# First chunk in halves of 64 times, own key's weight as a product, output banks from a second PSUM pool

## Chip, core and metric

One core of a Trainium2 chip runs the kernel. The metric is the device time of one execution in microseconds (us), the median of three runs. Besides, one execution was profiled; all rows below are from it.

## What is computed

Four sequences of 768 times with 8 heads of 48 channels go through a linear recurrence with a decaying state; the result goes, as 3072 tokens of 384 channels, through a two-layer network with a GELU between.

```
state = 0                                   # per batch and head, 48 x 48
for t in range(768):
    cur = (u * k[t]) outer v[t]             # the own key's weight is u
    y[t] = r[t] @ (state + cur)
    state = w[:, None] * state + k[t] outer v[t]
x = y as [3072, 384]
h = x @ w_in                                # 384 x 2048
out = (0.5 * h * (1 + erf(h / sqrt(2)))) @ w_out     # 2048 x 384
```

w_in and w_out come as 64-bit floats and are split on the chip into a high and a low part of 32 bits.

## The kernel before

**Tiling of the recurrence.** Time is cut into six chunks of 128. A chunk is four groups, one for each pair of heads; pair 3 comes first, since its channels fill the gaps of 16 rows in the other pairs' tiles (`x3`, `gaps`, `spread`). Within a chunk the recurrence is written as products: scores r times k with both sides scaled by powers of w, a mask that keeps past keys, the own key's weight on the diagonal, then the masked scores times v (`new`), r times the state (`old`), and the sum of k times v, weighted by powers of w, that updates the state (`gain`, `gains`).

**Two forms.** The first chunk (`first_group`, groups 0 to 3) takes all 128 times at once. It has no earlier state. Its tables `W` reach from w^-64 to w^64, with a reciprocal per pair (L271). T is scaled in up to two parts on VectorE (DVE) and GpSimd (POOL) (L393); r times k is formed per element (L399), summed per head with u by small products (`sum_pairs`, L404), brought out of PSUM (`cs`, L408) and put on the diagonal of `Am` by ScalarE (ACT), DVE or POOL (`bonus`, L351, L356); the scores (L419) are copied into `Am` where the mask says past (L425). `new` is L439, `gain` L445, and ACT copies the gain out as the state (L450). Groups 4 to 23 cut their 128 times into two halves of 64, each with its own state. They scale by `E` (L479), form r times k and times u on POOL (L482, L488), sum on DVE (L491), weight k by `WN2` on POOL (L485), and put the sums on the diagonals with eight ACT instructions (L351). `E` is filled from `W` by eight DMAs within SBUF (L303), because half 1 needs the heads of a pair swapped; `WN` and `WN2` are transposes by PE of two sets of powers (L290, L293).

```
def go():                  # one entry of PE's order per later group
    old()                  # r times state of the group before, into Y (L519)
    scores()               # scores of this group, into A (L527)
    gains()                # k times v of this group, into A beside the scores (L536)
    new()                  # masked scores times v of the group before, into Y (L546)
```

The state of a half is updated by DVE out of A (L569), the past scores are copied out of A (L576), and `keep` brings the output out of Y: ACT writes the high part (L367), DVE the low one (L368).

**The network.** 96 steps, 16 for each chunk of 512 tokens. In step m, `moe1` makes 128 hidden channels in bank `Hp` by nine products (high and low parts, L602), ACT applies GELU twice (L630, L631), DVE forms the low part (L632), and `moe2` of the step before adds nine products into the three output banks (L642). A pair of weights is loaded and split in the first 16 steps only (`w_split`: ACT L330, L332, L340; DVE L334, L336, L338, L342). The first `NEAR` weight tiles are there from the start; the others take the space of the first chunk's tiles, after `swap` has given back that pool.

**Order.** `Plan` holds every operation with its engine, a cost, a due time and what it reads and writes. It plays a model of the engines and fixes each engine's order before the program is built: of what is ready, the one due first. DMAs all go through the queue of SP. While PE would sit idle ahead of the first hidden product, the plan fills in products of zeros (`heat`), which keep its clock up.

**PSUM.** Eight banks: A (2), Y and U (one tile of 2 banks), Hp, and three output banks O. In the first chunk even groups use A and Y, odd ones O.

## Time and profile before

| what | value |
|---|---|
| median of three runs | 513.9 us (512.32, 513.9, 517.1) |
| the profiled execution | 512.43 us |
| its span, first to last instruction | 510.7 us |
| mean granted TensorE clock | 0.973 of 2.4 GHz |
| busy, share of the span | PE 96%, PEld 76%, DVE 49%, ACT 42%, POOL 17% |

PE is TensorE's products, PEld its weight loads, SPq the queue of SyncE that issues DMAs. A share of busy time is a mean over stages with different limits; the rows below go by stage. Products are pipelined, and the records of two that overlap both count, so a busy PE is not PE at its peak.

### The profile page before, as it was taken

How to read it: one execution, taken by the hardware profiler on the slowest of the kernel's cores; microseconds unless marked ns; L12 is line 12 of the kernel's file. 1: busy time of each engine (PE TensorE's matmuls, PEld its weight loads, DVE VectorE, ACT ScalarE, POOL GpSimd, SP SyncE). 2: the span in 40 equal slices, each digit the busy share in tenths (PEclk: the TensorE clock that was granted, in tenths of full speed). 3: DMA queues.
4: the chain of work that ended last, by engine and by line, in shares of the span. 5: the costliest groups of instructions: out<-in, count | busy, mean ns of one | idle time of the engine just before them, and what ended most of it. 6: DMA issues, size and time to landing. Idle time of an engine off the chain costs nothing.

```text
span 510.7 us, 10489 instructions
## 1 busy us (share of the span) xinstructions
PE 488.2 (96%) x4524; PEld 387.8 (76%) x4524; DVE 248.8 (49%) x363; ACT 213.6 (42%) x472; POOL 88.6 (17%) x80
## 2 busy tenths in 40 slices
PE   5998898999999999999999999999999999999995
PEld 4876676766778778787777778778778787888884
DVE  8959999998536424614425435424424311211111
ACT  2458758774444243333343443343442322322221
POOL 5850311213022022202022022022022000000000
PEclk8659999999999999999999999999999999999998
DMA  8864574822402303403302403303403000100001
GB/s 226 254 251 145 189 231 149 252 83 63 145 7 89 94 4 92 145 1 94 95 1 94 142 5 94 94 1 94 134 13 94 13 0 12 62 1 0 1 0 67
DMA packets 15107, 45.04 MB, mean 88 GB/s; under 512 B 3728, under 2 KB 4112, under 8 KB 15056
## 3 DMA queue, kind: packets, MB, share of 16 engines
q1 hardware_dynamic: 15056, 44.32, 27.8%
q8 instruction: 37, 0.61, 0.5%
q14 instruction: 14, 0.11, 0.1%
HBM read 37.16 MB, written 4.72 MB: 82 GB/s over the span
## 4 chain that ended last, share of the span: by engine, by line
PE 84%; DVE 11%; issue 2%; ACT 1%; DMA 1%; SPq 0%; DVEq 0%
PE Hp L602 37%; PE O L642 35%; PE Y L546 2%; PE Y L519 2%; PE A L527 2%; DVE wa L338 1%; DVE wl L342 1%; DVE Ts L393 1%; PE A L536 1%; PE Y L642 1%; DVE gl L632 1%; DVE wa L336 1%; DMA T<-in_rkT_dram 1%; DVE wa L334 1%; ACT wh L340 1%
## 5 line engine op out<-in xcount | busy, mean ns | idle before, releaser
L602 PE MATMUL Hp<-xx,wh 128*128 128x512 f32 x576 | 168.8, 400 | 0.8 <-ACT gf L631 0.5
L632 DVE TENSOR_TENSOR gl<-gf,gh 128x512 fp32r<-128x512 f32 x95 | 73.2, 770 | 193.9 <-ACT gf L631 193.8
L630 ACT ACTIVATE gh<-Hp 128x512 fp32r<-128x512 f32 x95 | 56.7, 597 | 183.6 <-PE Hp L602 183.5
L602 PEld LDWEIGHTS Hp<-xx,wh 128*128 128x128 f32 x576 | 105.8, 188 | 26.6 <-ACT gf L631 1.5
L642 PE MATMUL O<-gh,wh 128*128 128x512 f32 (+1 forms) x285 | 82.0, 395 | 6.2 <-ACT gh L630 6.2
L602 PE MATMUL Hp<-xx,wl 128*128 128x512 f32 x288 | 84.1, 399 | 0.7 <-DVE wl L342 0.3
L642 PE MATMUL O<-gh,wl 128*128 128x512 f32 (+1 forms) x285 | 80.8, 391 | 0.0
L642 PE MATMUL O<-gl,wh 128*128 128x512 f32 (+1 forms) x285 | 80.6, 390 | 0.0
L482 POOL TENSOR_TENSOR Nb<-Nb 128x384 f32<-128x384 f32 x20 | 22.6, 1131 | 294.9 <-DMA Nb<-in_rkv_dram 257.5
L642 PEld LDWEIGHTS O<-gh,wh 128*128 128x128 f32 x285 | 52.6, 188 | 23.4 <-ACT gh L630 11.9
L602 PEld LDWEIGHTS Hp<-xx,wl 128*128 128x128 f32 x288 | 53.5, 188 | 15.6 <-DVE wl L342 3.3
L642 PEld LDWEIGHTS O<-gl,wh 128*128 128x128 f32 x285 | 52.6, 188 | 11.9 <-DVE gl L632 0.2
L642 PEld LDWEIGHTS O<-gh,wl 128*128 128x128 f32 x285 | 52.6, 188 | 11.7
L351 ACT ACTIVATE Am<-diag,cs 128x64 f32<-128x64 f32 (+1 forms) x176 | 47.4, 345 | 22.8 <-DVE cs L491 22.7
L631 ACT ACTIVATE gf<-Hp 128x512 f32<-128x512 f32 x96 | 56.9, 593 | 0.0
L367 ACT CAST xx<-Y 112x512 fp32r<-112x512 f32 (+1 forms) x16 | 9.4, 587 | 41.7 <-PE Y L546 41.0
L479 DVE TENSOR_TENSOR Tb<-Tb,E 112x1024 f32<-112x1024 f32 x20 | 24.4, 1220 | 2.9 <-DMA Tb<-in_rkT_dram 2.9
L488 POOL TENSOR_TENSOR Nb<-Nb,u_sb 128x384 f32<-128x384 f32 x20 | 25.6, 1282 | 0.2
L569 DVE SCALAR_TENSOR_TENSOR Sb<-Sa,E,A 48x192 f32<-48x192 f32 x40 | 16.5, 413 | 16.0 <-PE A L536 15.4
L485 POOL TENSOR_TENSOR Nb<-Nb,WN 128x384 f32<-128x384 f32 x20 | 22.7, 1135 | 2.7 <-ACT WN L293 1.3
L576 DVE COPY_PREDICATED Am<-past,A 128x512 f32<-128x512 uint32 x20 | 14.8, 738 | 7.0 <-PE A L536 6.8
L342 DVE TENSOR_TENSOR wl<-wa,wh 128x768 fp32r<-128x768 f32 x16 | 16.7, 1042 | 1.9 <-ACT wh L340 1.7
(114 smaller groups left out, 396.1 us busy)
## 6 DMA issues: line engine op xcount, KB each, us to landing
raw<-in_wmlp_dram SPq DMA_DIRECT2D x16, 768.0 KB, 6.9
Nb<-in_rkv_dram SPq DMA_DIRECT2D x20, 576.0 KB, 5.4
Tb<-in_rkT_dram SPq DMA_DIRECT2D x20, 448.0 KB, 3.9
out_dram<-raw SPq DMA_DIRECT2D x5, 768.0 KB, 4.6
xx<-x SPq DMA_DIRECT2D x30, 64.0 KB, 3.9
T<-in_rkT_dram SPq DMA_DIRECT2D x4, 448.0 KB, 6.9
N<-in_rkv_dram SPq DMA_DIRECT2D x4, 384.0 KB, 9.5
out_dram<-raw SPq DMA_DIRECT2D x2, 256.0 KB, 2.8
```

What stands on the lines that cost most here:

```text
L342: add("dve", sdve(n), LATER, lambda: nc.vector.tensor_tensor(out=both(wl), in0=af, in1=both(wh).bitcast(F32), op=ALU.subtract), r=[A_, f"w ...
L351: add("act", sact(n) + 90, LATER, lambda b=b: nc.scalar.activation(out=am[:, j, b, :], in_=diag, func=AF.Copy, scale=sums[:, 2 * b + j:2 * ...
L479: add("dve", sdve(1024), LATER, lambda: nc.vector.tensor_tensor(out=flat, in0=flat, in1=E[:, 0, p].rearrange("l h i -> l (h i)").unsqueeze ...
L482: add("pool", pool(DM), LATER, lambda: nc.gpsimd.tensor_tensor(out=n[:, 0], in0=n[:, 0], in1=n[:, 1], op=ALU.mult), r=[NK], w=[NR])
L485: add("pool", pool(DM), LATER, lambda: nc.gpsimd.tensor_tensor(out=kn, in0=kn, in1=WN2[:, p].rearrange("s j d -> s (j d)").unsqueeze(1).to ...
L488: add("pool", pool(DM), LATER, lambda: nc.gpsimd.tensor_tensor(out=n[:, 0], in0=n[:, 0], in1=u_sb[:, p, :].unsqueeze(1).to_broadcast([C, N ...
L569: add("dve", 420, at, lambda l=l, x=x: nc.vector.scalar_tensor_tensor(out=out[quarter(1 - x)], in0=src[l], scalar=E[l, 1, p, h, 32:33], in ...
L602: nc.tensor.matmul(Hp, lhsT=wt[j][:, 0, k_ * 128:(k_ + 1) * 128], rhs=x[:, a, k_, :], start=start and k_ == ks[0], stop=stop and k_ == ks[-1])
L630: add("act", 480, LATER, lambda: nc.scalar.activation(out=high, in_=Hp, func=AF.Gelu), r=["H"], w=[GH])
L631: add("act", 480, LATER, lambda: nc.scalar.activation(out=gf, in_=Hp, func=AF.Gelu), r=["H"], w=["gf"])
L632: add("dve", dve(512), LATER, lambda: nc.vector.tensor_tensor(out=low, in0=gf, in1=high.bitcast(F32), op=ALU.subtract), r=["gf", GH], w=[GL])
L642: nc.tensor.matmul(dst[:, a:b], lhsT=wt[j][:, 1, d * 128:(d + 1) * 128], rhs=gt[:, a:b], start=(j == 0 and n == 0), stop=(j == NJ - 1 and ...
```

## The change

The first chunk takes the form of the later ones: halves of 64 times with a state each. Its scaling is one DVE instruction per group. All tables come from `E`, which reaches from w^-32 to w^31 and is made in place on DVE; `w` is loaded in both orders of a pair, so the DMAs from W to E go, and so does one of the two sets of transposes. In groups 0 to 7 (`DIRECT`) the own key's weight is a second product, of r with k scaled by u times w (`KB`, two ACT instructions), next to the scores in A, and a second masked copy puts it on the diagonal; r is no longer loaded for these groups in the layout of keys. The gains go into Y beside the output, and in `go` they follow `new`. Odd groups of the first chunk use four banks (AE, YE) of a second pool; when that pool is given back, its banks become the three output banks and Hp, each a tile of its own. Eight weight tiles in place of four are there from the start. The order of the loads changes, and the zero products pause at times (`hold`).

```diff
-NEAR = 4
+NEAR = 8
-LOADS = (1, 2, 3, "w0", "w1", "u", 4, 5, "w2")
+LOADS = (1, "w0", 2, 3, "w1", 4, 5, "w2", "u")
+DIRECT = 2 * NP
...
-        Hp = psp.tile([128, 512], F32, name="Hp")
-        O = [psp.tile([128, 512], F32, name=f"O{i}") for i in range(3)]
+        YU = psp.tile([128, 2, 512], F32, name="Y")
+        early_ps = ctx.enter_context(ExitStack())
+        pso = early_ps.enter_context(tc.tile_pool(name="pso", bufs=1, space=PSUM))
+        AE, YE = (pso.tile([128, 2, 512], F32, name=n) for n in ("AE", "YE"))
...
+        SETS = (((AA, ["A0", "A1"]), (YU, ["Y0", "Y1"])), ((AE, ["O0", "O1"]), (YE, ["O2", "H"])))
...
+            while n < MID:
+                m = min(n, MID - 1 - n)
+                times_one(E0[:, :, MID + n + 1:MID + n + 1 + m], E0[:, :, MID + 1:MID + 1 + m], one(E0, MID + n))
                 n *= 2
...
+            times_one(P32[:, 0].unsqueeze(2), one(E0, MID + 16), one(E0, MID + 16))
+            nc.vector.reciprocal(out=P32[:, 1], in_=P32[:, 0])
+            times_one(E0[:, :, 0:MID], E0[:, :, MID:HALF], P32[:, 1].unsqueeze(2))
...
+            times_one(E1[:, :, 0:MID], E0[:, :, MID:HALF], P32[:, 0].unsqueeze(2))
+            times_one(E1[:, :, MID:HALF], E1[:, :, 0:MID], P32[:, 0].unsqueeze(2))
...
-                nc.sync.dma_start(E[dst, a, :, h], W2[:, :, a, 0:HALF])
...
+            if g.direct:
+
+                for h in range(2):
+                    add("act", sact(256) + 90, LATER, lambda h=h: nc.scalar.activation(
+                        out=g.kb[:, :, times(h)], in_=g.t[:, 1, :, times(h)], func=AF.Copy,
+                        scale=uw[:, 2 * g.p + h:2 * g.p + h + 1]), r=[g.T, "uw"], w=[f"{g.KB}{h}"])
+                return
...
+        def own(g):
+            scores(g, g.kb, U0)
...
+        def first_group(gi):
+            g = Group(gi)
+            prepare(g)
+            add("pe", 600, LATER, lambda: scores(g), r=[g.T], w=g.X)
+            add("pe", 600, LATER, lambda: own(g), r=[g.T, f"{g.KB}0", f"{g.KB}1"], w=g.X)
+
+            def first_gains():
+                gains(g)
+                if gi % 2:
+                    plan.hold = True
+
+            add("pe", 500, LATER, first_gains, r=[g.K, g.V], w=g.Y)
+            state(g, 0, LATER)
+            select(g, diag2, "diag", U0)
+            select(g, past2, "past", 0)
+            if spreads(g):
+                add("pe", 1000, LATER, lambda: gaps(g), r=["spread", "x3h", "x3l"], w=g.Y)
+            add("pe", 1000, LATER, lambda: (old(g), new(g)), r=[g.T, g.V, g.AM] + g.S[1], w=g.Y)
+            keep(g, LATER)
+            state(g, 1, LATER)
+            if gi % 2:
+                add("do", 0, LATER, lambda: setattr(plan, "hold", False), w=g.Y)
...
             def go():
-                if prev is not None:
-                    old()
-                if gi is not None:
-                    scores()
-                    gains()
-                if prev is not None:
-                    new()
+                if g:
+                    old(g)
+                if f:
+                    scores(f)
+                    if f.direct:
+                        own(f)
+                if g:
+                    new(g)
+                if f:
+                    gains(f)
...
+        def banks():
+            plan.filler = None
+            early_ps.close()
+            later = ctx.enter_context(tc.tile_pool(name="psl", bufs=1, space=PSUM, reuse_waits="tile"))
+            O.extend(later.tile([128, 512], F32, name=f"O{i}" if i < 3 else "Hp") for i in range(4))
+
+        add("do", 0, 0, banks, w=["O0", "O1", "O2", "H"])
```

## Rows read from the trace of the kernel before

**Rows 1.** The page's 40 slices of 12.8 us: busy tenths of PE and DVE.
```profile
PE   5998898999999999999999999999999999999995
...
DVE  8959999998536424614425435424424311211111
```

**Rows 2.** Windows: us, then PE, PEld, DVE, ACT, POOL busy (instructions), granted clock, DMA share, GB/s.
```profile
0.00:25.00 25.00, 19.09 (x118) 16.07 (x120) 22.34 (x35) 8.52 (x26) 17.22 (x20) 0.75 0.84 236
25.00:35.00 10.00, 9.42 (x87) 7.24 (x85) 3.85 (x5) 5.70 (x13) 6.14 (x6) 0.50 0.94 342
35.00:46.00 11.00, 8.64 (x162) 6.47 (x162) 10.45 (x16) 8.56 (x22) 1.01 (x2) 0.94 0.23 76
46.00:128.50 82.50, 76.70 (x767) 55.47 (x757) 78.13 (x104) 59.12 (x109) 18.35 (x12) 1.00 0.50 162
128.50:504.00 375.50, 373.46 (x3411) 301.88 (x3410) 133.41 (x205) 131.33 (x306) 45.83 (x42) 1.00 0.18 55
```

**Rows 3.** Chain of waits, 100 to 135 us: start us, us, what.
```profile
124.23 0.96 DVE wl L342
...
128.56 2.10 PE Hp L602 x9
...
132.06 0.59 PE Y L519 x32
132.65 0.47 PE A L527 x32
133.12 0.36 PE A L536 x32
133.48 0.14 issue
133.62 0.67 PE Y L546 x32
```

**Rows 4.** Groups of instructions, DVE, 0 to 46 us: busy us, mean ns, idle before.
```profile
L393 DVE TENSOR_TENSOR Ts<-T,W 112x512 f32<-112x512 f32 (+1 forms) x4 | 7.2, 1816 | 0.9 <-DMA T<-in_rkT_dram 0.9
...
L479 DVE TENSOR_TENSOR Tb<-Tb,E 112x1024 f32<-112x1024 f32 x2 | 2.4, 1220 | 0.0
L271 DVE RECIPROCAL W<-W 112x64 f32<-112x64 f32 x4 | 1.9, 520 | 0.0
...
L285 DVE TENSOR_TENSOR W<-W,P 112x128 f32<-112x128 f32 x1 | 1.4, 1352 | 0.0
...
L399 DVE TENSOR_TENSOR RK<-T 112x512 f32<-112x512 f32 x1 | 1.3, 1274 | 0.0
...
L281 DVE COPY W<-W 112x128 f32<-112x128 f32 x1 | 1.1, 1109 | 0.0
...
L569 DVE SCALAR_TENSOR_TENSOR Sb<-Sa,E,A 48x192 f32<-48x192 f32 x2 | 0.8, 414 | 0.1
```

**Rows 5.** Timeline of DVE, then of POOL, 53 to 66 us.
```profile
55.73 1.77 DVE L342 TENSOR_TENSOR wl<-wa,wh 128x768 fp32r<-128x768 f32 x1
...
55.07 1.62 POOL L485 TENSOR_TENSOR Nb<-Nb,WN 128x384 f32<-128x384 f32 x1
```

**Rows 6.** Groups of instructions, PE, 0 to 46 us.
```profile
L404 PE MATMUL Hp<-wu_sb,RK 112*128 112x2 f32 x32 | 4.9, 274 | 1.2 <-POOL RK L399 1.2
L419 PE MATMUL A<-Ts 64*128 64x128 f32 (+1 forms) x32 | 4.2, 423 | 0.1
...
L439 PE MATMUL O<-Am,N 128*48 128x128 f32 x32 | 3.7, 406 | 0.0
```

**Rows 7.** Timeline of SP's queue, 0 to 130 us.
```profile
13.33 9.14 SPq L303 DMA_DIRECT2D E<-W  x8
```

**Rows 8.** Timeline of ACT, 33 to 48 us.
```profile
36.08 0.64 ACT L450 COPY Sa<-Y 48x192 f32<-48x192 f32 x2 [0.40 <-DVE xx L368]
...
40.01 2.02 ACT L351 ACTIVATE Am<-diag,cs 128x64 f32<-128x64 f32 x8
...
43.34 0.60 ACT L630 ACTIVATE gh<-Hp 128x512 fp32r<-128x512 f32 x1
```

More of the change, by code (lines that the diff above doesn't have):

```diff
@@ L110, in run @@
                 fill, buf, ns, room = self.filler
-                while not unread and max(free[e], clear) + room < start:
+                while not unread and not self.hold and max(free[e], clear) + room < start:
                     fill()
@@ L123, in run @@
             if self.filler:
-                unread += sum(self.filler[1] in self.reads[m] for m in users[n])
+                unread += sum(self.filler[1] in self.reads[m] for m in users[n] if self.ops[n][0] == "pe")
                 if self.filler[1] in self.reads[n]:
@@ L314, in rwkv_gelu_mlp @@
+        add("act", 500, LATER, lambda: nc.scalar.copy(
+            out=WN, in_=AE[:, 1].rearrange("s (p j x) -> s p j x", p=NP, x=64)[:, :, :, :D]), r=["O1"], w=["WN"])
         wbits = wmlp.bitcast(I32)
@@ new lines, in scores @@
+        def scores(g, keys=None, col=0):
+            for b in range(NB):
+                for h in range(2):
+                    for x in range(2):
+                        k_ = (g.t[:, 1] if keys is None else keys)[quarter(x), b, times(h)]
+                        nc.tensor.matmul(g.x[times(h), x, col + b * HALF:col + (b + 1) * HALF], lhsT=k_,
+                                         rhs=g.t[quarter(x), 0, b, times(h)], start=True, stop=True)
+        def own(g):
+            scores(g, g.kb, U0)
@@ new lines, in gains, with old @@
+        def gains(g):
+            for b in range(NB):
+                for x in range(2):
+                    for h in range(2 if g.more else 1):
+                        nc.tensor.matmul(g.y[quarter(x), h, U0 + b * D:U0 + (b + 1) * D], lhsT=g.kn[times(h), b, heads(x)],
+                                         rhs=g.vn[times(h), b, heads(x)], start=True, stop=True)
+        def old(g):
+            for b in range(NB):
+                for j in range(2):
+                    for h in range(1 if g.c == 0 else 0, 2):
+                        l = quarter(j ^ h)
+                        nc.tensor.matmul(g.y[quarter(j), h, b * HALF:(b + 1) * HALF], lhsT=g.s[h][l, b, :],
+                                         rhs=g.t[l, 0, b, times(h)], start=(b == 0 and not spreads(g)), stop=False,
+                                         skip_group_check=True)
@@ new lines, in new @@
+        def new(g):
+            nc.tensor.drain()
+            for b in range(NB):
+                for j in range(2):
+                    for h in range(2):
+                        nc.tensor.matmul(g.y[quarter(j), h, b * HALF:(b + 1) * HALF], lhsT=g.vn[times(h), b, heads(j ^ h)],
+                                         rhs=g.am[times(h), j ^ h, b, :], stop=True, skip_group_check=True,
+                                         start=(g.c == 0 and h == 0 and b == 0 and not spreads(g)))
+        spreads = lambda g: g.c == 0 and g.p < 3
@@ new lines, in select, with keep @@
+        def select(g, mask, MASK, col):
+            add("dve", 722, LATER, lambda: nc.vector.copy_predicated(
+                out=g.am, mask=mask.bitcast(U32).unsqueeze(1).unsqueeze(1).to_broadcast([C, 2, NB, HALF]),
+                data=g.x[:, :, col:col + U0].rearrange("s x (b t) -> s x b t", t=HALF)),
+                r=[f"{MASK}20", f"{MASK}21"] + g.X, w=[g.AM])
+        def keep(g, at):
+            xt, XT = xx[g.c % 2], f"xx{g.c % 2}"
+            p = g.p
+            l = slice(0, 128 if spreads(g) else LP)
@@ L371, in keep @@
-            if p < 3 and rows == LP:
+                out=view(dst[l, 1]), in0=src, in1=view(dst[l, 0].bitcast(F32)), op=ALU.subtract),
+                r=g.Y + [f"{XN}h"], w=[f"{XN}l"])
+            if p < 3 and not spreads(g):
                 for j in range(2):
@@ new lines, in group @@
+        def group(gi, at):
+            f = Group(gi) if gi < NG else None
+            g = Group(gi - 1) if gi > NP else None
+            if f:
+                prepare(f)
+            products(g, f)
+            if f:
+                state(f, 0, LATER)
+                if f.direct:
+                    select(f, diag2, "diag", U0)
+                select(f, past2, "past", 0)
+            if g:
+                keep(g, at)
+            if f and f.more:
+                state(f, 1, at + 20000)
@@ L667, in moe2 @@
             last = m == NSTEP - 1
-            for i, (d, bank, a, b) in enumerate(parts):
+            for i, (d, dst, a, b) in enumerate(parts):
                 o, R = (raw[i], f"raw{i}") if last and i < 3 else (N[NP], f"Nr{NP}") if last else (raw[0], "raw0")
@@ L761, in rwkv_gelu_mlp @@
         for gi in range(NP):
[L762 to L764 removed]
+            first_group(gi)
         def swap():
```

441 lines of the change are left out of this document (142 added, 299 removed).

## The prediction

> **What bounds the kernel now.** I read the 40 slices first [rows 1]. Each is 12.8 us. TensorE (PE) is at 9 from the eighth slice to the last but one, while VectorE (DVE) is at 8 or 9 in nine of the first ten and at 1 to 6 behind them. So there are two regimes, and the windows [rows 2] put numbers on them: from 46 to 128.5 us DVE is busy 78.13 of 82.50 us, and from 128.5 to 504 us PE is busy 373.46 of 375.50.
>
> The chain of waits [rows 3] says where one becomes the other. The last low part of a weight pair (wl, L342) ends at 125.2, the first step of the second chunk begins at 128.56, and from there the chain is matmuls end to end: nine of 2.10 us for the hidden layer, nine for the output, and every fourth step a block of recurrence products (0.59 + 0.47 + 0.36 + 0.14 + 0.67 us). Behind 128.56 no saving on DVE, ScalarE (ACT), GpSimd (POOL) or DMA counts, only PE's own work. Ahead of it 16 steps take 91 us. PE alone would need 16 x 4.2 + 5 x 2.2 = 78, so it has about 13 us of slack, and DVE's queue (first chunk, then sixteen weight splits) sets the pace. The question is by how much DVE reaches the last split sooner.
>
> Up to 46 us DVE is busy 22.34 + 3.85 + 10.45 = 36.6 us [rows 2], so idle for 9.4, of which 6.15 lie between 25 and 35 us. There PE is 94% busy at a granted clock of 0.50, which is the 1.2 GHz level: DVE waits for products.
>
> **The change part by part.** The sum is made against the profiled execution: 510.7 us of span and 1.73 around it, 512.43. The median of the three runs, 513.9, is 1.5 above that.
>
> DVE's work up to 46 us [rows 4]. The four scalings of T (L393, 7.2 us, with POOL doing two parts beside them) become four instructions of L479's form, 112x1024 at 1.22: 4.9, so -2.3. Four reciprocals (L271, 1.9) become one of eight elements per lane; from 0.52 for 64 I take 0.2: -1.7. The product r times k on DVE (L399) goes: -1.3. L281 and L285 (1.1 + 1.4) go, and three products over 256 elements come; scaled from L479 these are 0.3 plus a fixed part, I take 0.4 each: -1.3. Small instructions on both sides (single powers, uw, the masked diagonals) I set against each other. New are eight state updates for the second half of the first chunk, L569's form, 8 x 0.41 = +3.3. The selects stay eight. Sum: -3.3.
>
> Collisions with POOL [rows 5]: the same subtraction (L342) took 1.77 us beside a POOL product and 0.96 without one [rows 3], so one POOL product can cost DVE 0.81. The long L393, L399 and L285 above hold such losses, and they go with the POOL products that caused them (parts of the scaling, r times k, diagonals). What stays are six weightings of k by WN (groups 0 to 5): nothing to 6 x 0.81 = 4.9. I take 1.5, nearer to nothing, since six products leave DVE free for most of the stretch. By the Trainium skill's page "SBUF — State Buffer", section Who interferes with whom, a DVE instruction with two SBUF inputs is blocked for the whole of a GpSimd instruction that reads SBUF, and one with a single SBUF input is not; the row agrees in kind, but shows half of the POOL product's 1.62 us lost and not all of it. By that rule the six would cost nothing where they meet selects, whose data lies in PSUM, and up to 6 x 1.62 = 9.7 where they meet scalings: an estimate of 502 to 512 for the time.
>
> DVE's idle time up to 46 us. PE's sets per group at 1.2 GHz, before [rows 6]: sums of pairs 4.9/4 = 1.2, scores 4.2/2 = 2.1, new products 3.7/2 = 1.85, together 5.2. After: scores, own, old (half a set) and new, with the times of rows 3, taken at 2.4 GHz, doubled: 2 x (0.47 + 0.47 + 0.3 + 0.67) = 3.8. Gains and gap products keep their columns. That is -1.4 a group, -5.6 in all, and one of two sets of transposes goes. The eight copies from W to E, which hold the SP queue from 13.33 on [rows 7], go too, and the transfers queued behind them (T and N of groups 4 and 5, then a weight) are issued earlier; the scaling that needs them stands behind DVE's own queue, so I count nothing. So PE, which DVE waited for, ends the first chunk 5 to 6 us sooner even if it stays at 1.2 GHz. I put the idle time at 4 in place of 9.4: -5.4 (bounds: 2.7 left, which is what 0 to 25 us has now, and 9.4).
>
> Edits beside the path. First hidden product: it now waits for the second PSUM pool, so for the last reader of groups 1 and 3. All its nine matmuls come behind that, where six came before the last group's product; that is +1.4 us on PE, covered by its slack of 13. On ACT the eight diagonal activations of a group (2.02 us [rows 8]) become two; before, gh of the first step stood behind such a group and came only at 43.34. The own-key product adds 0.47 us to PE in four calls, all ahead of 128.56 and so under the same slack. The loads in another order, eight near weights in place of four, and the two clears of Am on POOL before any data has landed: nothing; of the four pairs that are free of the early pool only two are split by 46 us, and the pool is given back with the first chunk's end.
>
> The ramp, groups 6 and 7: two of three POOL products go in each, 4 x 0.81 = -3.2 at most; a second select stands against the reduction that goes; ACT's six activations fewer free a few of DVE's short waits. I take -2.3 (bounds -3.2 and 0). Groups 8 and up are as before.
>
> A new wait: state updates (DVE) and the kept output (ACT, then DVE) now read the same tile Y, where the updates read A. In this trace an ACT copy out of one bank of Y sat idle for 0.40 us until a DVE read of the other bank was over, with no data between them [rows 8]. So reads of one tile by two engines follow each other. Queued behind a waiting update are DVE's weight splits. Nothing to 0.8 us for each of the five calls in the ramp; I take 0.2 each: +1.0.
>
> Behind 128.56: 16 calls with the order old, scores, new, gains in place of old, scores, gains, new. The pause of the drain was 0.14 [rows 3]; it can grow or shrink by that: 0, bounds -2.2 and +2.2.
>
> Sum: -3.3 + 1.5 - 5.4 - 2.3 + 1.0 = -8.5, so 512.43 - 8.5 = 503.9; against the median, which lies higher, I say 504.3.
>
> **The rivals.** First: the first chunk stays a chain of hand-overs at 1.2 GHz. For it: the 25 to 35 us window is that already. Each group gets four more links: two scaled key copies on ACT (0.4 each, above the 0.32 of a state copy of 192 columns), own (0.94), the two state copies (0.64 [rows 8]) and the old product, 0.6, some 3.0; two groups overlap, so +6.0 over four, which eats the 5.6 that PE saves. Idle rises by 0.4, and what is left is -3.3 + 1.5 + 0.4 - 2.3 + 1.0 = -2.7: 510. Against it: ACT and DVE have fewer instructions between the links, and POOL leaves the chain.
>
> Second, slower: the reads of Y. If the kept output's copy stands ahead of the updates, DVE waits for new (0.67), gains (0.36), ACT's current instruction and the copy (0.6 each, as gh [rows 8]), 2.2 us, in nine calls up to the last split: 20 us, against 9.5 saved without this term. It decides from 9.5/9 = 1.06 us a call; at 1.8 it is +6.7: 519. For it: the 0.40 us row. Against it: DVE's updates can as well come first, and then ACT waits, which has room. [...]
>
> Third: the change speeds the first chunk, but the ramp turns out to hang on ACT or PE. ACT is busy 59.12 of 82.50 us [rows 2], and PE's 78 us would start some 5 us sooner, so neither ends last before about 13 us are gained. This caps the gain and makes no case of its own.
>
> **How the numbers follow.** Forecast, 504: chance 0.68. Chain of hand-overs, 510: 0.20. Reads of Y, 519: 0.12. All terms at their good ends give -3.3 - 6.7 - 3.2 - 2.2 = -15.4: 497, and 498 is the low end, since they will hardly all come. The high end takes in the first rival and its bounds, 511.5, and leaves out the second and little else. One per cent, 5 us, is about what a measurement of this kernel tells from no change. Faster by more 0.68, within it 0.20, slower 0.12.
>
> **What would show it.** Right: DVE's idle time over the same work falls to about 4 us, that work ends near 39 in place of 46, the first step of the second chunk begins near 120 in place of 128.56, and the stretch behind it keeps its length. The first rival shows as DVE gaps released by PE or ACT between 15 and 35 us; the second as gaps ahead of the updates, released by ACT's copy. The sum is wrong if PE's clock stays at 0.5 into the weight steps, or if the blocks of products behind the ramp change by more than 0.14 us each.

## The result, and the profile after

The changed kernel took **518.08 us** (median of 16 runs, 515.81 to 519.98), the kernel before 513.91 (16 runs beside it): ratio 1.0078, 95% interval [1.0053, 1.0104]. It is slower by 0.8%, where the prediction said 504.3 us in a range from 498 to 511.5. The profiled executions took 519.95 us (span 517.9) and 512.43 (span 510.7). Here and below the ratios leave out the few executions that fell into a slower state (in e3 two of ten), so a ratio need not be that of the two medians.

The windows come first, with the stretches of [rows 2] and the same columns:

```profile
0.00:25.00 25.00, 15.28 (x347) 12.95 (x348) 14.57 (x30) 10.59 (x23) 6.13 (x14) 0.69 0.93 269
25.00:35.00 10.00, 6.92 (x155) 5.96 (x155) 3.57 (x7) 2.32 (x5) 1.99 (x2) 0.50 0.56 181
35.00:46.00 11.00, 10.35 (x120) 7.79 (x122) 8.69 (x13) 5.50 (x10) 0.00 (x0) 0.50 0.01 2
46.00:128.50 82.50, 75.33 (x955) 56.30 (x955) 75.07 (x106) 52.41 (x78) 8.07 (x6) 0.99 0.51 167
128.50:511.00 382.50, 379.75 (x3438) 306.28 (x3437) 143.13 (x212) 136.20 (x320) 49.52 (x44) 1.00 0.18 54
```

Up to 25 us every engine but ACT is less busy than before: DVE 14.57 in place of 22.34, POOL 6.13 in place of 17.22, and PE 15.28 in place of 19.09, although PE has 347 matmul records there in place of 118. Up to 46 us it has 620 in place of 357. The products are much smaller, there are more of them, and the engines stand idle for longer.

The landmarks say where the loss lies. The second weight pair's low part (L326, L342 before; called the second split below) ends at 52.6 us in place of 46.0, the sixteenth at 130.4 in place of 125.2, the first output is issued at 139.73 in place of 133.19, the last at 511.94 in place of 505.41. So 6.6 us are lost ahead of the second split, and from the first output on both kernels take 372.2 us. Between the two, the ramp up to the sixteenth split takes 77.8 us in place of 79.2, but from there to the first output it is 9.4 in place of 8.0: what the ramp gained is gone again. So the loss is that of the first chunk. Its chain of waits (start us, us, what):

```profile
9.06 1.24 DVE T L357
...
14.54 0.73 PE Y L409 x13
15.27 2.76 issue
18.03 0.45 PE Y L409 x3
18.56 1.11 PE Y L419 x32
19.67 1.71 PE AE L390 x64
21.37 0.83 PE A L390 x27
22.20 4.65 issue
26.85 0.48 PE A L390 x5
27.33 1.15 PE YE L429 x4
28.48 1.02 PE YE L409 x16
...
33.01 0.41 PE YE L401 x6
33.41 0.32 issue
33.74 0.87 PE YE L401 x26
...
42.11 3.78 PE Hp L544 x8
```

"issue" is time in which PE waited for nothing that the profile shows. Three such gaps stand in the chunk, 7.73 us together, and each is in the **middle of a row of equal products**: after 13 of the 16 old products of group 0, after 27 of 32 scores of group 2, after 6 of 32 gains of group 3. The products behind the gap need no data that those ahead of it did not. In the kernel before PE has no idle time without a releaser that is longer than 0.15 us, the least that the views list.

The gaps are evenly spaced in instructions. From the end of the first to the start of the second stand 3 + 32 + 64 + 27 = 126 matmul records, from the second to the third 127 (5 + 4 + 16 + 32 + 32 + 32 + 6), each with a weight load beside it in the rows of PEld: some 252 to 254 instructions, and a drain per group. Two smaller gaps without a releaser, of 0.99 us at 54.11 and 0.68 at 77.16, stand in the ramp. Counted from the start of the trace, the five stand behind 221, 347, 474, 855 and 1109 matmul records: one spacing of 126 or 127, or a multiple of it. An fp32 product is two records: 64 of them, added to the kernel before (below), show as x128. The page of the changed kernel has a DMA queue of its own for this, and a window of 1 us in the second gap shows one of its packets:

```profile
q8 instruction: 41, 0.67, 0.6%
...
q8 instruction: 1, 0.02, 8.1%
```

41 packets of 0.67 MB in all are 16 KB each. In 1 us windows they come at 15, 24 and 31 us, and the three gaps end at 18.03, 26.85 and 33.74, 2 to 3 us behind the packet. The Trainium skill's page "Runtime: NRT & Kernel Launch", section Instruction fetch mechanics, says that the sequencer refills its memory through a DMA queue of its own in blocks of 16 KiB, 256 instructions; the spacing and the packets agree. It also says that the cost of crossing such a block is mostly hidden; here it is 2.76 and 4.65 us in the open.

What DVE makes of it, in its timeline (last column: idle before, and what ended it):

```profile
20.35 0.41 DVE L442 SCALAR_TENSOR_TENSOR Sa<-Sb,E,Y 48x192 f32<-48x192 f32 x1 [3.22 <-ACT x L461]
30.77 0.41 DVE L442 SCALAR_TENSOR_TENSOR Sa<-Sb,E,YE 48x192 f32<-48x192 f32 x1 [7.26 <-PE YE L419]
31.83 0.42 DVE L442 SCALAR_TENSOR_TENSOR Sa<-Sb,E,YE 48x192 f32<-48x192 f32 x1 [0.65 <-ACT xx L461]
39.52 0.69 DVE L462 TENSOR_TENSOR xx<-YE,xx 128x512 fp32r<-128x512 f32 x1 [2.14 <-ACT xx L461]
```

Waits of 3.22 and 7.26 us end right behind the outputs that PE's two long gaps delayed. Up to the second split DVE is busy 32.02 of 52.6 us, where it was 36.6 of 46: its work fell by 4.6 us and its idle time rose from 9.4 to 20.6. The rows that answer to [rows 4], DVE's groups up to 52.6 us (busy, mean ns, idle before), show the fall:

```profile
L357 DVE TENSOR_TENSOR T<-T,E 112x1024 f32<-112x1024 f32 x4 | 4.9, 1220 | 4.0 <-DMA T<-in_rkT_dram 4.0
...
L276 DVE RECIPROCAL P<-P 112x8 f32<-112x8 f32 x1 | 0.2, 203 | 0.0
```

The scaling and the reciprocal cost what the prediction gave them, and at 1220 ns a scaling shows nothing lost to POOL. None ran beside a POOL product: POOL's weightings of k fell into DVE's idle time or beside selects of 0.73 us.

### The profile page after: what moved, and what is told of

The parts are those of the page before. It is cut to its first block, busy times and chain, and to the rows that moved or that the text cites. A ratio compares the mean times of both kernels' runs of the same rounds, so it can differ in the third digit from the quotient of the medians.

```text
span 517.9 us, 11402 instructions
## 1 busy us (share of the span) xinstructions
PE 488.1 (94%) x5006; PEld 389.5 (75%) x5006; DVE 245.5 (47%) x366; ACT 207.1 (40%) x435; POOL 65.7 (13%) x66
## 4 chain that ended last, share of the span: by engine, by line
PE 85%; DVE 6%; issue 3%; DMA 3%; ACT 1%; POOL 1%; SPq 0%; POOLq 0%
PE Hp L544 37%; PE O L585 35%; PE Y L419 3%; PE A L390 3%; PE Y L409 3%; PE Y L401 1%; DMA Nb<-in_rkv_dram 1%; DMA T<-in_rkT_dram 1%; DVE wl L326 1%; PE Y L585 1%; DVE wa L322 1%; DVE Sa L442 1%; PE AE L390 1%; ACT gh L572 1%; DVE gl L574 1%
## 5 line engine op out<-in xcount | busy, mean ns | idle before, releaser
L574 DVE TENSOR_TENSOR gl<-gf,gh 128x512 fp32r<-128x512 f32 x95 | 75.9, 799 | 183.4 <-ACT gf L573 183.2
L585 PEld LDWEIGHTS O<-gh,wh 128*128 128x128 f32 x285 | 52.6, 188 | 19.6 <-ACT gh L572 7.8
L585 PEld LDWEIGHTS O<-gl,wh 128*128 128x128 f32 x285 | 52.6, 188 | 11.8 <-DVE gl L574 0.2
L585 PEld LDWEIGHTS O<-gh,wl 128*128 128x128 f32 x285 | 52.6, 188 | 11.6
L361 POOL TENSOR_TENSOR Nb<-Nb 128x384 f32<-128x384 f32 x16 | 21.0, 1315 | 262.5 <-DMA Nb<-in_rkv_dram 227.2
L381 ACT ACTIVATE Am<-diag,cs 128x64 f32<-128x64 f32 x128 | 33.9, 342 | 27.6 <-DVE cs L376 27.6
L442 DVE SCALAR_TENSOR_TENSOR Sb<-Sa,E,Y 48x192 f32<-48x192 f32 x40 | 16.5, 413 | 35.4 <-ACT xx L461 28.0
L363 POOL TENSOR_TENSOR Nb<-Nb,WN 128x384 f32<-128x384 f32 x20 | 21.5, 1076 | 59.3 <-DMA Nb<-in_rkv_dram 58.1
L447 DVE COPY_PREDICATED Am<-past,A 128x512 f32<-128x512 uint32 x22 | 16.2, 736 | 8.9 <-PE A L390 6.0
L373 POOL TENSOR_TENSOR Nb<-Nb,u_sb 128x384 f32<-128x384 f32 x16 | 17.7, 1106 | 0.1
L326 DVE TENSOR_TENSOR wl<-wa,wh 128x768 fp32r<-128x768 f32 x16 | 17.4, 1089 | 0.2
```

Of the source, the lines that this page charges most:

```text
L326: add("dve", sdve(n), LATER, lambda: nc.vector.tensor_tensor(out=both(wl), in0=af, in1=both(wh).bitcast(F32), op=ALU.subtract), r=[A_, f"w ...
L361: add("pool", pool(DM), LATER, lambda: nc.gpsimd.tensor_tensor(out=g.n[:, 0], in0=g.n[:, 0], in1=g.n[:, 1], op=ALU.mult), r=[g.K], w=[g.R])
L363: add("pool", pool(DM), LATER, lambda: nc.gpsimd.tensor_tensor(out=g.kn, in0=g.kn, in1=WN[:, g.p].rearrange("s j d -> s (j d)").unsqueeze( ...
L381: add("act", sact(HALF) + 60, LATER, lambda x=x, b=b: nc.scalar.activation(out=g.am[:, x, b, :], in_=diag2, func=AF.Copy, scale=g.sums[:, ...
L442: add("dve", 420, at, lambda l=l, x=x, more=more: nc.vector.scalar_tensor_tensor(out=g.s[h + 1][quarter(1 - x)], in0=g.s[h][l], scalar=E[l ...
L574: add("dve", dve(512), LATER, lambda: nc.vector.tensor_tensor(out=low, in0=gf, in1=high.bitcast(F32), op=ALU.subtract), r=["gf", GH], w=[GL])
```

## The experiments

Three theories stand in the expectations. **Supply**: PE runs out of instructions at the end of a block, because the next comes by DMA behind bulk loads. **Clock**: the small products leave PE at 1.2 GHz, and that is the loss. **Hand-over**: outputs and updates read one tile in turn, and the chain of small steps is the loss. Ratios are to the kernel before, with 95% intervals.

### Loads held back

The DMA engines were full (share 1.03 or more) at the two long gaps, with weights and groups 4 and 5 that the first chunk doesn't need. Held back, they leave the queue to the instructions. One element of each target is written first by POOL, from a tile that is ready late:

```diff
+        HELD = ('w1', 'w2', 4, 5)
+
+        def hold_back(dst, tags):
+            add("pool", 120, LATER, lambda: nc.gpsimd.tensor_copy(out=dst, in_=x3[0:1, 0, 0:1].bitcast(F32)), r=["x3h"], w=tags)
...
```

They are held until group 0's output is kept (e1), or until group 1's (e2, `xx[0]` in place of `x3`); e6 is e2 with the first weight held as well, until group 0's output:

> The changed kernel, with the second and third weight pair and the loads of groups 4 and 5 held back until group 0's output is kept. Supply theory (PE runs out of instructions at the end of a block of 256, because the next block comes by DMA behind these loads): the gap of 4.65 us in PE's products falls below 1.5 us, the one of 2.76 us stays within 1 us, the low part of the second weight pair ends near 49 in place of 52.6 us, and the time is 1 to 5 us below the changed kernel's. Clock theory (the small products leave PE at 1.2 GHz, and this is what costs): the gap may go, but PE waits elsewhere instead, and the time stays within 1 us of the changed kernel's. Hand-over theory (outputs and updates reading one tile in turn): as the clock theory.

> As the run before it, but held back until group 1's output is kept, some 6 us later. Supply theory: the 4.65 us gap is gone as well (below 1 us), the second weight pair and group 4 come later, so the time lies between the run before and the changed kernel. Clock and hand-over theories: not below the changed kernel's time, and up to 3 us above it for the late weights.

> The changed kernel with the first weight held back until group 0's outputs are kept, and the second and third weight and groups 4 and 5 until group 1's are. Supply theory: less is moved while the first block of instructions is fetched, so the first gap falls from 2.76 us (3.23 where all but the first weight were held back) to 2 us or less and the later ones stay as where all but the first weight were held back; but the first weight itself comes later, which can cost as much: 515 to 517 us. Clock theory and hand-over theory: no change in the gaps, 518 or later since weights come later.

Measured: e1 517.69 us, 1.0064 [1.0026, 1.0102]; e2 516.05, 1.0031 [1.0002, 1.0061]; e6 516.44, 1.0050 [0.9991, 1.0110]. e1 is 0.4 us below the changed kernel, where the supply theory expected 1 to 5; e2 was expected between the two and is below both. All three intervals overlap with the changed kernel's, so the gaps in the traces carry the argument, and not the times. PE's timeline of e2 (the same records on both sides of each gap as in the changed kernel):

```profile
17.70 0.45 PE L409 MATMUL Y<-T,Sb 48*48 48x64 f32 x3 [3.23 <-issue]
18.23 1.11 PE L419 MATMUL Y<-Am,N 64*48 64x64 f32 x32
19.10 1.08 PE L390 MATMUL AE<-T 48*64 48x64 f32 x32
19.96 1.08 PE L390 MATMUL AE<-T,KB 48*64 48x64 f32 x32
20.81 1.06 PE L390 MATMUL A<-T 48*64 48x64 f32 x27
22.13 0.48 PE L390 MATMUL A<-T 48*64 48x64 f32 x5 [0.26 <-issue]
```

This is the cleanest pair of the study. The same 126 records stand between the two gaps. With the DMA engines full, PE took 26.85 - 18.03 = 8.82 us from one block to the next; with them idle, 22.13 - 17.70 = 4.43. The packet itself came late: in the microsecond from 24 us in the changed kernel, 6.0 us behind the end of the gap before it, and in that from 19 us in e2, 2.3 us behind. The windows around it, first of the changed kernel, then of e2 (the last two columns are DMA share and GB/s):

```profile
10.00:16.00 6.00, 4.88 (x173) 4.70 (x173) 4.08 (x7) 3.08 (x8) 2.01 (x2) 0.50 1.04 300
19.00:25.00 6.00, 3.20 (x119) 3.02 (x111) 3.04 (x5) 3.78 (x6) 0.00 (x0) 0.50 1.03 274
```

```profile
10.00:16.00 6.00, 4.28 (x173) 4.16 (x173) 4.25 (x7) 3.08 (x8) 2.02 (x2) 0.72 1.04 311
19.00:22.00 3.00, 2.87 (x105) 2.69 (x98) 1.90 (x4) 2.61 (x5) 0.00 (x0) 0.50 0.03 10
```

The clock is at 0.50, its 1.2 GHz level, on both sides of the pair, so the clock doesn't tell them apart. In e1 the held loads start sooner; the gap at the third block, 0.32 us in the changed kernel, becomes 2.33 at a DMA share of 1.02, while the second falls from 4.65 to 0.54 (share 0.10 from 18 to 21 us, where its packet came). The gap went where the loads went.

The first gap stayed in all three: 2.48, 3.23 and 3.80 us. In e6 that was against the expectation. The windows give the reason: with or without the first weight the loads of groups 0 to 3 fill the engines until 16 us (share 1.00 in e6 from 15 to 16). So e9 holds the loads of groups 2 to 5 and all weights until the weights of group 0's keys are selected:

```diff
+        HELD = (2, 3, 'w0', 'w1', 'w2', 4, 5)
...
+            add("pool", 120, LATER, lambda: nc.gpsimd.tensor_copy(out=dst, in_=Am[0][0:1, 0, 0, 0:1]), r=["Am0"], w=tags)
...
```

> The changed kernel with the loads of groups 2 to 5 and of all three weights held back until group 0's weights are selected (some 14 us), so that the DMA engines are idle while TensorE's first block of instructions runs out; in every run so far they were full until 16 us and the first gap without releaser was 2.5 to 4.8 us. Supply theory: the first gap (end of the row of old products of group 0) falls to 1 us or less; a later gap, while the held loads run, is 1.5 us or more; the time is later than the changed kernel's, since groups 2 and 3 and the weights come some 8 us later: 520 to 528 us. Clock theory and hand-over theory: the first gap stays 2.5 us or more.

```profile
13.31 1.06 PE L409 MATMUL Y<-T,Sb 48*48 48x64 f32 x16
...
26.69 1.11 PE L390 MATMUL A<-T,KB 48*64 48x64 f32 x26 [0.98 <-issue]
...
35.56 0.45 PE L419 MATMUL Y<-Am,N 64*48 64x64 f32 x3 [1.51 <-issue]
```

```profile
9.00:14.00 5.00, 3.86 (x174) 3.89 (x176) 3.42 (x5) 1.94 (x6) 1.90 (x9) 0.71 0.07 18
21.00:26.00 5.00, 3.92 (x134) 3.39 (x130) 3.72 (x5) 2.48 (x8) 1.35 (x1) 0.50 1.03 356
31.00:35.00 4.00, 2.96 (x77) 2.53 (x77) 2.48 (x4) 0.58 (x1) 1.60 (x2) 0.50 1.02 309
```

The first gap is gone at a DMA share of 0.07: the sixteen old products run in one piece. The two later gaps stand where the loads are back, 127 records apart. The time, 514.51 us in one run, is below the 520 to 528 expected: in that run loads that come 8 us later cost less than the gaps that went.

Five kernels do the same products and differ in held loads alone. Wherever one of them stops by 0.2 us or more, it is behind 221, 347, 474, 601, 855 or 1109 records, to within one. All gaps without releaser up to 131 us, and the span of the same execution:

| kernel | gaps, us | span, us |
|---|---|---|
| the change | 9.40 | 517.9 |
| e1 | 7.08 | 515.0 |
| e6 | 6.91 | 515.6 |
| e2 | 5.22 | 514.1 |
| e9 | 2.49 | 512.8 |

A least-squares line through them gives 0.71 us of span for each us of gap and 510.6 us at no gap, against 510.7 for the kernel before. That is an extrapolation from single executions: the spans of the changed kernel alone run from 514.0 to 517.9 in its 16, and with each kernel's median time in place of the span the line has a slope of 0.53. It holds for these five only (e15, below, leaves it), but for them the gaps are about the size of the whole loss.

### More instructions, and a faster clock, in the kernel before

64 tiny products (e3), or seven products of zeros (e4), behind group 0's sums:

```diff
+                if gi == 0:
...
+                    for _ in range(64):
+                        nc.tensor.matmul(O[1][0:32, 0:2], lhsT=zf[:, 0:32], rhs=zf[:, 0:2], start=True, stop=True)
```

```diff
+                if gi == 0:
+                    for _ in range(7):
+                        nc.tensor.matmul(O[1], lhsT=zeros[:, 0:128], rhs=zeros, start=True, stop=True)
```

> The kernel before, with 64 more products of zeros, 32 x 2 (256 instructions), in PE's idle time from 8.3 us on. Supply theory: PE reaches the end of a block earlier, while the loads fill the DMA engines, and gets a gap of 1 to 5 us with no releaser in the middle of a row of equal products between 12 and 22 us; the time rises by 1 to 4 us over before. Clock and hand-over theories: no such gap, time within 1 us of before.

> Control for the run before it: the kernel before, with 7 more products of zeros of 128 x 512 at the same place (3 us of PE, but 14 instructions). Supply theory: no gap without a releaser, time within 1 us of before. Clock theory: PE's clock stays at 2.4 GHz for longer than 9.5 us, and the time may fall by 0 to 2 us.

e3: 517.73 us, 1.0034 [0.9993, 1.0075], and no gap without releaser:

```profile
7.82 6.99 PE L409 MATMUL O<-zeros 128*32 128x2 f32 x128
```

The 64 products, 128 records, took 6.99 us, within the 4.43 to 8.82 us from block to block above, so PE may have used them up no faster than they came. The expected gap failed to show, and this doesn't speak for supply; as a test it is inconclusive.

e4: 512.91 us, 0.9994 [0.9962, 1.0026]. The clock stood at 1.00 up to 36 us where it had been 0.50 from 20 to 36:

```profile
20.00:36.00 16.00, 12.76 (x164) 9.57 (x162) 15.29 (x17) 9.39 (x21) 11.60 (x10) 1.00 0.71 243
```

The second split ended at 43.0 in place of 46.0, the last output was issued at 504.01 in place of 505.41. So the low clock of the whole first chunk was worth 3 us at the split and 1.4 us at the end, too little to tell in the times. In the kernel before, then, the low clock isn't worth the size of the loss; that it isn't the main cause in the changed kernel is argued from this, and not shown.

The same seven products in the changed kernel behind group 0's scores, with the loads as in e2 (e7) and as in e9 (e13):

> The changed kernel with the second and third weight and groups 4 and 5 held back until group 1's outputs are kept, and with seven products of zeros (128x512) behind the scores of group 0, which keep TensorE busy while it waits. Clock theory: the granted clock stays at 1.0 through the first chunk, the small products take half of their time, and the second weight pair is split 4 us or more sooner than the 48.1 us of the same kernel without them: 511 to 513 us. Supply theory: products at the full clock use up their blocks of instructions sooner, so the gaps without releaser grow by about what the products save; the pair is split at 46 to 49 us, 514 to 517 us.

> The changed kernel with the loads of groups 2 to 5 and of all weights held back until group 0's weights are selected (one run of which took 514.51 us, gaps 0.98 and 1.51), and seven products of zeros behind the scores of group 0. Clock theory: with the first gap gone the clock can stay at 1.0 as it did in the kernel before with the same products; the second split then ends 3 us or more before the 49.0 us without them, as it ended 3.0 sooner in the kernel before: 510 to 512 us. Supply theory: faster products meet the ends of their blocks sooner, with 2.4 to 3.4 us from one block's start to the next at the least, and gaps of 1 us or more come at each: the split ends within 1.5 us of 49.0, 513 to 516 us.

e7: 518.17 us, 1.0091 [1.0033, 1.0149]; e13: 515.24, 1.0052 [1.0029, 1.0075]. Neither gained, and e7 is above what either theory expected. In e7 the first gap grew to 4.62 us, since PE, at full clock, used up its block sooner; the clock then fell in the gap. In e13, where the second split ended at 48.6 (49.0 in e9), the clock fell at 16 us all the same. What the changed kernel would do at full clock throughout stays open.

### Parts of the change undone

**The own key's weight left out** (e5), the product, its scaled keys and its select, in groups 0 to 7:

```diff
-            add("pe", 600, LATER, lambda: own(g), r=[g.T, f"{g.KB}0", f"{g.KB}1"], w=g.X)
...
-            select(g, diag2, "diag", U0)
```

> The changed kernel without the own-key product, the scaled copies of the keys on ScalarE and the select that puts its diagonal in, in all eight groups: it leaves the own key's weight out of the result. That is 16 products of four instructions per group less, 256 instructions up to the end of the first chunk and 256 behind. Supply theory: TensorE meets the end of a block of 256 instructions once less up to 52 us, so the gaps without a releaser (2.76, 4.65, 0.32, 0.99 us in the changed kernel) become one fewer or move, the second weight pair is split 5 us or more sooner than at 52.6 us, and of that more than the 0.7 us of PE and 0.8 us of DVE per group that the work itself takes; 510 to 514 us. Clock theory: the own-key products are a sixth of the small products at the low clock; 1 to 2 us sooner, 515 to 517. Hand-over theory: one link less per group (a scaled copy and a select), 0.5 to 1 us a group where two overlap, so 2 to 4 us: 514 to 516, with the gaps without releaser left as they are.

511.30 us, 0.9952 [0.9896, 1.0009]; the second split at 46.2 in place of 52.6. Two gaps, 3.45 and 2.66 us, in place of three:

```profile
14.30 0.73 PE L386 MATMUL AE<-T 48*64 48x64 f32 x28
18.47 0.48 PE L386 MATMUL AE<-T 48*64 48x64 f32 x4 [3.45 <-issue]
```

The place bears out the count. The own products of groups 0 and 1, 64 records, are gone ahead of the first gap, and it stands 64 records later in the order of the rest: behind the last 3 old products, 32 new ones and 28 scores (63 in the trace). Counted from the start, the two gaps of e5 stand behind 220 and 346 records, the first two of the changed kernel behind 221 and 347. Of the 6.4 us at the split, 1.6 are gap (7.73 to 6.11) and 4.4 are PE's busy time (33.49 in place of 37.87 us; part of that is the clock, which rose at 41.8 us in place of 46.9). So with 6.11 us of gap left e5 is level with the kernel before: the gaps aren't all of the loss, and the own products' time on PE counts beside them.

**By sums in groups 4 to 7** (`DIRECT = NP`), with the loads as in the change (e8), as in e2 (e10) and as in e9 (e15):

> The changed kernel with the own key's weight by product in the first chunk alone: groups 4 to 7 get it as in the kernel before, by two products on GpSimd, a sum on DVE and eight scaled diagonals on ScalarE. That undoes one part of the change. Up to the first hidden product nothing changes but the order of work. Supply theory: 64 instructions fewer in each of groups 4 to 7, so the gaps in the ramp (0.99 at 55 us, 0.68 at 77 us) go or move; against that the ramp has GpSimd's products back (0.81 us of DVE each, 4 to 8 in it, and what the prediction took for them: 2.3 us). 517 to 521 us; it cannot win back more than 2 us, since the whole loss stands ahead of 52 us. Clock theory says the same of the time and nothing of the gaps.

> The changed kernel with the second and third weight and groups 4 and 5 held back until group 1's outputs are kept, and with the own key's weight by product in the first chunk alone. Supply theory: the gaps up to the second split stay as with the held loads alone (3.49 us in all), the ramp as with the own key's weight by sums in groups 4 to 7 (2 us shorter than the changed kernel's): 512 to 515 us, which is level with the kernel before. Clock theory and hand-over theory: 516, since the loads change nothing for them.

> The same held loads, with the own key's weight by product in the first chunk and by sums in groups 4 to 7. Up to the second split as with the held loads alone (49.0 us, gaps of some 2.5 us in all); the ramp 1.5 to 2.5 us shorter than the changed kernel's: 511 to 514 us. By the prediction's own terms the sums cost the ramp 2.3 us more than the products: 516 to 518.

e8: 516.22 us, 1.0065 [1.0002, 1.0128]; e10: 515.05, 1.0027 [1.0005, 1.0048]; e15: 518.05, 1.0096 [1.0061, 1.0132]. e8 is below the 517 to 521 expected. Its ramp took 75.5 us in place of 77.8 and has no gap, where the changed kernel has 0.99 and 0.68; e10's took 77.2 in place of e2's 79.9, with none of e2's gaps of 1.48 and 0.25. So in groups 4 to 7 the own key's product made the ramp longer, by 2.3 and 2.7 us, of which 1.7 are gaps. Beside e9, whose ramp has no gap, it is the other way: 76.8 with the products, 77.9 with sums (e15). e15 was a miss: its only gap is 1.22 us, yet its span is 516.4, while e8, with gaps of 10.34 us, has 514.8. In e15 the second split ended at 51.6, only 1.4 ahead of e8's, and the ramp took 77.9 us in place of e8's 75.5. The first hidden product waited for the weights there (1.41 us for ACT's high part, 0.88 for DVE's low one). So where the held loads bring the weights late, that is the next limit, and the gaps alone don't set the time. Why the ramps of e8 and e15, the same code, differ by 2.4 us was not settled.

**By sums in all eight groups**, so that only the halves and the output banks are left of the change (e11); with the loads as in e2 (e12); by sums in groups 2 to 7 with the loads held as in e9 (e14, which also loads u early); and e11 with w and groups 0 and 1 loaded ahead of u (e16). e11's edit begins so:

```diff
-LOADS = (1, "w0", 2, 3, "w1", 4, 5, "w2", "u")
-DIRECT = 2 * NP
+LOADS = ("u", 1, "w0", 2, 3, "w1", 4, 5, "w2")
+DIRECT = 0
...
```

> The changed kernel with the own key's weight by sums in all eight groups (GpSimd products, a sum on DVE, scaled diagonals on ScalarE), so that only the halves of 64 times and the output banks are left of the change; u is loaded first. Supply theory: TensorE's instructions are those of the run without own-key products, so the gaps without releaser are about its 6.1 us in all and its 511.3 us is the bound; GpSimd's eight further products in the first chunk cost DVE up to 0.81 us each: 512 to 517 us. Hand-over theory: GpSimd's two products (1.6 us each), the sum and eight activations (2 us) stand in each group's chain in place of the 0.9 us product and its two copies: later than the changed kernel, 519 to 523 us. Clock theory: 517.

> As the run with sums in all eight groups, with the second and third weight and groups 4 and 5 held back until group 1's outputs are kept. Supply theory: the gaps fall to some 3.5 us as they did with the products, so 2 us below the run without the held loads: 509 to 514 us. Hand-over theory and clock theory: as the run without the held loads.

> As the run with the loads of groups 2 to 5 and all weights held back until group 0's weights are selected, with the own key's weight by product in groups 0 and 1 alone and by sums in groups 2 to 7. 64 products and 256 instructions fewer in the first chunk, one block, and the shorter ramp that the runs with sums in groups 4 to 7 had (2 to 4 us). Supply theory: one gap is left up to the second split, 1.5 us or less; the split ends 2 to 3 us before 49.0 and the time is 508 to 512 us, faster than both kernels. Hand-over theory: two GpSimd products, a sum and eight activations stand in the chain of groups 2 and 3, so nothing is gained ahead of the split: 512 to 515 us.

> The changed kernel with the own key's weight by sums in all eight groups, as in the run that took 512.39 us, but with w and the loads of groups 0 and 1 issued first and u behind them. Supply theory: TensorE's scores of group 0 begin near 7.3 us as in the changed kernel (13.68 in that run), the gaps without releaser are those of the run without own-key products or fewer (6.1 us at most), and the time is 509 to 512 us, below both kernels. If the sums' own chain (GpSimd, ScalarE) paces the first chunk, the earlier start is lost and it stays at 512 to 514 us.

e11: **512.39 us**, 0.9970 [0.9946, 0.9995]; e12: 512.94, 0.9984 [0.9962, 1.0007]; e14: 513.25, 1.0009 [0.9982, 1.0036]; e16: **512.23 us**, 0.9976 [0.9947, 1.0004]. e11 has one long gap left, 4.01 us; e12 has none over 0.59 and is no faster, against the expectation. e14, for which one gap of 1.5 us or less was expected, has 0.88, 2.44 and 0.80. e16 has none over 0.55 either, and its PE shows why that doesn't help:

```profile
13.24 1.06 PE L407 MATMUL Y<-T,Sb 48*48 48x64 f32 x16
21.00 1.10 PE L417 MATMUL Y<-Am,N 64*48 64x64 f32 x32 [6.70 <-DVE Am L445]
```

PE waits 6.70 us for group 0's weights, which now hang on POOL's products, DVE's sum and ACT's diagonals. ACT's diagonals end at 18.25 us; DVE's select of group 0 begins only at 20.22, behind two scalings that waited 2.07 and 0.21 us for their loads. So in e16 the chain of hand-overs, with these loads in DVE's queue, sets the pace of the first chunk; the second split ends at 49.2 us there, at 49.5 to 50.5 in the other three. All four still beat the changed kernel, by 0.7 to 1.1%, and e11 and e16 stand 0.3 and 0.2% below the kernel before, e11 with an interval that leaves 1 out by little. Read as a split of the change, the halves and the banks are worth about -0.3% and the own-key product about +1.1%; e11 has another order of loads too, and whether the two parts add up was not tested.

## Why the prediction was wrong

**The step that failed** is "DVE's idle time up to 46 us", with "So PE, which DVE waited for, ends the first chunk 5 to 6 us sooner even if it stays at 1.2 GHz" and its term of -5.4. The first chunk's last output products ended at 40.88 us in place of 36.74 in the timeline of before, and DVE's idle time up to the second split went to 20.6 us in place of 4. That is 4.1 of the 6.6 us; the rest comes behind these products, where the first hidden step ran at the low clock (below). The step failed three times over.

*A price that was missing.* Products were costed by their time alone. PE's instructions up to the second split more than doubled (785 matmul records up to 52.6 us in place of 357 up to 46), and with some 127 records to a block the blocks came too late under the bulk loads: 7.73 us in the chunk. Shown by the pair 8.82 against 4.43 us for the same records, by the first gap that goes with the load (e9), and by the gap that moves by 64 records when 64 are taken out (e5).

*Two savings that can't be added.* DVE's work was summed at -3.3 + 1.5 and came out at -4.6, better than forecast. But where DVE waits for PE, less work for DVE is more waiting. Even in e9, with gaps of 2.49 us, DVE was busy 33.3 us and idle 15.7 up to the second split at 49.0. The end of such a stretch is PE's, and one of the two terms should have stood alone.

*What PE itself saved.* The sets of a group were priced rightly: 3.8 forecast, and 0.85 (scores) + 0.85 (own) + 1.02 (old) + 1.15 (new) = 3.87 measured at 1.2 GHz, though old alone took 1.02 where 0.6 was forecast: half a set of it costs nearly a whole. The 5.2 of before was too high, since [rows 6] mixes stretches at either clock. From 10.39 us, where its row of products becomes dense, to the last output PE was busy about 21.9 us (30.5 less gaps of 7.73 and a wait of 0.81); before, from 12.29, it was 23.9 (24.45 less a wait of 0.58). That is 2 us saved, and not 5.6. The clock, too, stayed at 0.50 until 46.9 us where it had risen at 36.4, so eight products of the first hidden step took 3.78 us in place of some 2.

**Where the prediction also went past a cause.** [rows 7] were read as a pure gain: the copies from W to E held SP's queue until 22.5 us. They also held back groups 4 and 5 and a weight. "I count nothing" for these loads, which the change brings earlier, left out a cost: they are the loads that delayed the block at 24 us (e1, e2). That the queue held up by the copies spared the kernel before a gap is not shown. Its DMA share fell to 0.52 at 20 us, when a packet of the instruction queue came, but the next packet came at 39 us only, which is more than twice the 8.82 us above. So a later packet would hardly have cost anything; this is argued from the packets, not tested.

**A row read wrongly.** In [rows 5] the subtraction began 0.66 us into the POOL product, when 0.96 us of it were left. It lost 0.81 us of these 0.96; the prediction read this as half of the product's 1.62. Of the 1.5 us that the prediction put in for such collisions the first chunk showed nothing, since the weightings met no scaling.

**What held, and what was luck.** Behind the ramp: 0 forecast, and 372.2 us in both kernels. DVE's scaling and tables as priced. The ramp agrees by luck: -1.3 forecast (-2.3 + 1.0), -1.4 measured at the sixteenth split. The -2.3 stood for the products in place of POOL's work in groups 6 and 7, and where the ramp had gaps the products made it longer (e8, e10, with groups 4 to 7); and the 1.4 us are gone by the first output. In the kernel before PE's last wait for a low part ends at 125.23 us, at the sixteenth split; in the changed kernel the last ends at 115.37, and behind that PE waits 0.69 us for ACT and for nothing else of 0.15 us or more up to the first output. So there the end of the ramp is PE's, and the sixteenth split is no longer the landmark. That is the third rival's sign, though nothing like 13 us had been gained. The own-key product's cost behind the first chunk, "covered by its slack of 13", was not covered in full, by the same runs.

**The rivals.** "Reads of Y" gave 519 us, close to what was measured, but not for its reason: the waits of an update for ACT's copy of the same tile are there, 0.65 us at 31.83 and the last 0.7 of the 3.22 at 20.35, beside the 0.40 of [rows 8], and not the 1.8 a call on which the 519 rests; the loss is over before the ramp, where five of its nine calls stand. The chain of hand-overs was given 510 us. Its sign did show: DVE's gaps of 3.22 and 7.26 us between 15 and 35 us were released by ACT and PE. But what lay behind them is PE's stop in the middle of a row, and not a link of the chain; the chain showed as a limit in e16. That the change makes PE wait for its own instructions was not among the cases.

What stays open: the share of the low clock in the changed kernel, why its ramp ends on PE, and the last 3 us of the second split in e9, where the gaps are small and the split still ends behind that of the kernel before.

## What to carry to other kernels

When an edit cuts products into smaller ones, count the instructions as well as the time: here some 127 fp32 matmul records, which PE ran through in 2 to 4 us, used up a block of instructions, and that was a limit where bulk loads filled the DMA engines in the same stretch. Look for idle time without a releaser in the middle of a row of equal instructions, and check its spacing; then ask which loads in that stretch nobody needs yet. In a stretch where engine A waits for engine B, only B's saving counts.

## What the runs showed of the hardware

- PE's stops without a releaser stood behind the same counts of matmul records in five kernels that differ in their loads alone (221, 347, 474, 601, 855 and 1109, to within one), and at 220 and 346 where 32 products (64 records) were taken out ahead of the first (e5).
- The next block of PE's instructions took up to 8.82 us from the start of the one before with the DMA engines full (share 1.03), and 4.43 us, mostly PE's own work, with them idle (0.03).
- Even with little traffic small fp32 products at the full clock run into it. Below, from 52 to 54 us, PE runs through 128 records in 1.89 us at a DMA share of 0.33; at 54.11 it stops for 0.99 us, with a packet of the instruction queue at 52 us. This is a window of the changed kernel:

```profile
52.00:54.00 2.00, 1.89 (x128) 1.74 (x117) 2.00 (x4) 0.94 (x1) 0.00 (x0) 1.00 0.33 51
```
